# Packed attention and mixer on one core: making the last batch's packs among the first batch's products

## The chip, the cores and the metric

The kernel runs on one core of one Trainium2 chip. The metric is the device time of one execution in microseconds (us). Its engines are named as the profile names them: PE (TensorE, matmuls; PEld is its weight load), DVE (VectorE), ACT (ScalarE), POOL (GpSimd) and SP (SyncE, from whose queue all the DMAs of this kernel are issued).

## The reference

Eight batches, eight heads, 576 tokens, head dimension 64; 32 packing queries per head. Attention is done twice: the packing queries attend to keys and values and give 32 packed vectors per head, and then the real queries attend to the packed vectors. What comes out is mixed over the tokens with two thin matrices, and goes through a two-layer channel product with a relu.

```python
def _attn_ref(q, k, v, p):            # q, k, v: (8, 8, 576, 64), p: (8, 8, 32, 64)
    p_packed = sm_attn(p, k, v)       # softmax(p k^T / 8) v
    return sm_attn(q, p_packed, p_packed)

def _moe_ref(x, U, V, w_ch1, w_ch2):  # x: (8, 576, 512)
    h = x.transpose(0, 2, 1) @ U @ V  # U: (576, 32), V: (32, 576)
    u = x + h.transpose(0, 2, 1)
    ch = np.maximum(u @ w_ch1, 0.0) @ w_ch2   # (512, 2048), (2048, 512)
    return u + ch
```

U, V, w_ch1 and w_ch2 come as float64 bits; the kernel makes float32 of them on ACT and DVE.

## The kernel before, in words

**Units and packs.** The first attention is done in 16 units u = 0 to 15, two per batch, four heads each (`UN`). A unit goes through these steps, each a function: `a_load` (keys, and the packing queries with the first unit of a batch), `a_load_v` (values), `a_p` (packing queries turned, once per batch), `a_turn` (keys turned by ten PE transposes, copied out of PSUM), `a_scores` (matmuls into two banks), `a_softmax` (maximum on DVE, exponential with its sum on ACT), `a_turn_back` (five transposes of the exponentials, copied by ACT and DVE), `a_pack` (matmuls with the values; L470), `a_heads` (one transpose, and the packed vectors go to DRAM with the second unit of a batch). The loop at L505 runs these in a staggered order: in turn i it does turning back of i-1, scores of i, the turning of i+1, the pack of i-2 and the heads of i-3. Between them it converts the first weight matrix in 16 pieces and, from i = 4 on, does three steps a turn of the first batch's second attention.

**The second attention and the products.** `attention(b, res)` gives a list of 24 steps for batch b: one load of the queries, turning and scores and softmax of two halves, three steps `tokens`, `mix1` and four `mix2`. Each PE step takes one or two of two PSUM banks (pool psT, `bank()`), shared by everything. The last, `mix2`, does a matmul, an addition on DVE (L329), a copy on ACT (L330) and a subtraction on POOL (L331), and gives the pair of tiles ah and al which the products read. `fold(b, c)` multiplies a quarter of the first weight matrix by the packed vectors: eight matmuls into both banks of psT (L368), then four copies on ACT (L374) and four subtractions on DVE (L375).

The main loop (L678) runs over 8 batches and 16 rounds kt. A round is `gemm1(kt)` (12 matmuls, L86 to L88, into h_ps; relu on ACT, the low half hl on DVE at L607) and `gemm2(kt-1)` (12 matmuls into o). Products are made with three matmuls each, of high and low parts. Into a round are put: a step of the next batch's attention after `gemm1` (slot A), one after `gemm2` (slot B, where in every fourth round the fold stands instead), and in batch 0, one step between the halves of `gemm2` (slot M) for what is left of the packs. In batch 0 each round also converts one block of the second weight matrix (`load_w2`, `convert_w2`, `split_w2`): one operation on ACT, four on DVE (L78 to L81), a copy on ACT (L158) and a subtraction on POOL (L159).

**What sets the order.** Up to the line `tc.manual_schedule()` (L552) a planner orders each engine's instructions by a simulated time, so that in the first part steps may stand in another order than the code has them. Behind that line the instructions of each engine stand in the order in which the code issues them, and a slot's step waits in its engine's queue for what it needs. Tiles are in pools with a fixed count of buffers; a new tile waits until the old one of its buffer is read. The pool sA holds the keys, psA six banks of PSUM; both are closed at L548, and the products' tiles and banks take their place. sT stays open until the last `a_heads`.

Before the change all 16 units are turned, scored and exponentiated in the loop; three things are left for batch 0's slots M (`rest`, L542): the packs of units 14 and 15, the turning back of unit 15, the heads of 13, 14 and 15.

Of the kernel before, what the change touches and what calls it, by code (L numbers as in the profile page):

```python
# [8 lines left out]
F32 = mybir.dt.float32  # L9
# [10 lines left out]
def packed_attention_mixer_kernel(  # L20
# [28 lines left out]
    B, H, S, D = q.shape  # L49
# [4 lines left out]
    P = 128  # L54
    SM = 512
    NT = 9
    I = S // NT
# [98 lines left out]
    def split_w2(kt, x):  # L156
        hi, lo = w2_parts(kt)
        nc.scalar.copy(hi, x)  # L158
        nc.gpsimd.tensor_tensor(lo, x, hi.bitcast(F32), op=ALU.subtract)  # L159

    ua4 = const.tile([P, 5, 4, R], F32R, name="ua4")
    vs = const.tile([P, S], F32R, name="vs")
    nc.gpsimd.memset(ua4[I:, 4].bitcast(F32), 0.0)

    def x_tile():
        return pipe.tile([P, 5 * 2 * P], F32, name="x", tag="x", bufs=2)

    def load_uv():  # L170
        ub = x_tile()[:, :10 * R].bitcast(I32)
# [60 lines left out]
    def scores(lT, t, g, bank):  # L232

        ss = [bank() for _ in range(2)]
        for x in range(4):
            hs, h = slice(32 * x, 32 * x + 32), x ^ g
            for r in range(2):
                rs = slice(64 * r, 64 * r + 64)
                n = HALF[r].stop - HALF[r].start
                nc.tensor.matmul(ss[r][hs, :n], lhsT=lT[rs, g, hs], rhs=t[rs, h, :n], start=True, stop=True)  # L240
        return [ss[r][:, :HALF[r].stop - HALF[r].start] for r in range(2)]
# [10 lines left out]
    def attention(b, res):  # L252
# [10 lines left out]

        def turn_q(g, h):
            if h == 0:
                st["t", g] = pipe.tile([P, 4, 5 * I], F32, name="xT", bufs=1)
            turn(st["t", g], st["x", g], h, bank)

        def scores_q(g):
# [114 lines left out]
    sA = actx.enter_context(tc.tile_pool(name="sA", bufs=2, reuse_waits="tile"))  # L384
    psA = actx.enter_context(tc.tile_pool(name="psA", bufs=2, space=PSUM, reuse_waits="tile"))

    UN = [(b, g) for b in range(B) for g in range(2)]
    ua = {}
    pn, pT, pps = {}, {}, {}
# [4 lines left out]
    def a_load(u):  # L394
        b, g = UN[u]
        ua[u] = {}
        if g == 0:
            pn[b] = sA.tile([P, 2, 2, D], F32, name="pn")
            for z in range(2):
                nc.sync.dma_start(out=pn[b][:, :, z], in_=p[b].rearrange("(g h) n d -> (h n) g d", g=2))  # L400
        ua[u]["x"] = sA.tile([P, 2 * S], F32, name="kx", bufs=3)
        load_nat(ua[u]["x"], k, b, g)

    def a_load_v(u):
# [7 lines left out]

    def a_p(b):
        t_ps = bank()
        pT[b] = sA.tile([P, 2, P], F32, name="pT")
        for i in range(2):
            nc.tensor.transpose(t_ps[:, P * i:P * i + P], pn[b][:, i].rearrange("p z d -> p (z d)"), ident)
        nc.scalar.activation(pT[b][:, 0], t_ps[:, :P], AF.Copy, scale=scale)
        dst, src = (a.rearrange("p (y z n) -> p z y n", y=2, z=2) for a in (pT[b][:, 1], t_ps[:, P:2 * P]))
        for z in range(2):  # L420
            nc.scalar.activation(dst[:, z], src[:, 1 - z], AF.Copy, scale=scale)
# [6 lines left out]
        for h in range(3):  # L428
            turn(ua[u]["t"], ua[u]["x"], h, bank_a("k"))

    def a_scores(u):
        b, g = UN[u]
        ua[u]["s"] = scores(pT[b], ua[u]["t"], g, bank_a("s"))

    def a_softmax(u):
        ss = ua[u]["s"]
        mx = sA.tile([P, 3], F32, name="mx")
        sm = ua[u]["sum"] = sT.tile([P, 2], F32, name="sm", bufs=3)
        for r in range(2):
            nc.vector.tensor_reduce(mx[:, r:r + 1], ss[r], axis=AX.X, op=ALU.max, negate=True)  # L440
        nc.vector.tensor_tensor(mx[:, 2:], mx[:, :1], mx[:, 1:2], op=ALU.min)
        e1 = ua[u]["e"] = sT.tile([P, S], F32, name="e1")
        for r in range(2):
            nc.scalar.activation(e1[:, HALF[r]], ss[r], AF.Exp, bias=mx[:, 2:], accum_out=sm[:, r:r + 1])
# [57 lines left out]
            load_w1(n + 4)  # L502

    n_w1 = 0
    for i in range(NU):  # L505
        if i > 0:
            a_turn_back(i - 1, bank_a("m"))
        a_scores(i)
        if i + 1 < NU:
            a_load_v(i + 1)  # L510
            a_turn(i + 1)
        if i + 2 < NU:
            a_load(i + 2)
        a_softmax(i)
        for _ in range(2 if i in (1, 5, 9) else 1):
            if n_w1 < 16:
                some_w1(n_w1)
                n_w1 += 1
        if i > 1:
            a_pack(i - 2, bank_a("m"))  # L520
        if i > 2:
            a_heads(i - 3)
        if i >= 4:
            for _ in range(3):
                if first:
                    first.pop(0)()
        if i == 2:
            uv = load_uv()
        if i == 3:
            prepare_uv(*uv)  # L530
        if i == 12:
            load_w2(0)
            load_w2(1)
        if i == 13:
            fold(0, 0)
            steps = attention(1, res)
            steps.pop(0)()
        if i == 14:
            split_w2(*convert_w2(0))
            load_w2(2)  # L540
    assert not first
    rest = [  # L542
        lambda: (a_pack(NU - 2, bank), a_heads(NU - 3)),
        lambda: a_turn_back(NU - 1, bank),
        lambda: (a_pack(NU - 1, bank), a_heads(NU - 2)),
        lambda: (a_heads(NU - 1), tctx.close()),
    ]
    actx.close()  # L548
    split_copies = False

# [120 lines left out]
            nc.sync.dma_start(out=out[b - 1 + i].rearrange("(i c) m -> c i m", c=NT)[8], in_=os_[I * i:I * i + I])  # L671

    w2x = convert_w2(1)

    for n in (16, 15, 15, 12):
        steps.insert(n - 1, lambda: None)
    last, parts = None, []
    for b in range(B):  # L678
        cur = Batch(b)
        oj = None  # L680
        ahead = attention(b + 2, res) if b + 2 < B else []
        for kt in range(NK):
            cur.gemm1(kt)
            if oj and kt == 1:
                store_joint(b - 1, oj)
            if steps and (b == 0 or kt % 4 != 2):
                steps.pop(0)()
            if (b, kt) == (0, 5):
                w2_tiles(ctx.enter_context(tc.tile_pool(name="sC", bufs=1, side="right", reuse_waits="tile")), 2)
            if kt > 0:  # L690
                cur.gemm2(kt - 1, rest.pop(0) if rest else None)
            elif last:
                last.gemm2(NK - 1)
                last.store()
                if last.b % 2 == 1:
                    oj = joint(last.b, parts)
            if w2x:
                split_w2(*w2x)
                w2x = None
                if kt + 3 < NK:  # L700
                    load_w2(kt + 3)
                if kt + 2 < NK:
                    w2x = convert_w2(kt + 2)
            if kt % 4 == 2 and (b, kt) != (B - 1, NK - 2):
                n = b * NPC + kt // 4 + 1
                fold(n // NPC, n % NPC)
            elif steps:
                steps.pop(0)()
            if kt == 1:
                cur.blocks()  # L710
            if kt == 3:
                cur.add_u()
            if ahead and kt == 13:
                ahead.pop(0)()
            if kt == NK - 1 and b % 2 == 1:
                parts = [joint_parts(b, 0), joint_parts(b, 1)]
        assert not steps
        steps = ahead
        last = cur
# [35 lines left out]
```

## Time and profile before

| | |
|---|---|
| runs shown | 871.92, 868.63, 870.24 us; median 870.24 |
| the profiled execution | 869.67 us, of which the span of instructions is 867.1 |
| mean granted TensorE clock | 0.98 |
| DMA moved | 59.09 MB, mean 68 GB/s |
| PE / DVE / ACT / POOL busy | 829.0 / 391.6 / 330.2 / 99.3 us |

The chain of work that ended last is 82% PE, 8% DVE, 6% DMA and 2% ACT. The profile cuts the span into stretches and gives each engine's busy time in each: the first 121 us, in which packs are made and weights are converted, differ from the rest, in which the matmuls of the products follow each other. In a row of the timeline the columns are the start, the duration, the engine, the line, the operation, the tile written and the tiles read, partitions x elements, and how many; in brackets stand the idle time of the engine just before it and what ended it. A row of the waits names the waiting engine and line, what it waited for, the total, the count and the longest. A row of the chain has start, time, engine, tile and line.

### The profile page before, as it was taken

What the parts mean: (1) busy time and instruction counts of PE and PEld (TensorE: products, weight loads), DVE (VectorE), ACT (ScalarE), POOL (GpSimd) and SP (SyncE); (2) the same over time, 40 slices, a digit from 0 to 9 for tenths busy, and PEclk for the clock granted to TensorE, in tenths of its full rate; (3) what the DMA queues carried; (4) which work ended last, traced back from release to release, by engine and by line L of the source; (5) the groups of instructions that cost most, each with busy time, mean ns of one, the idle gap of its engine ahead of it and who ended that gap; (6) DMA issues with size and microseconds to landing.
All of it is one profiled execution on the core that took longest, in us unless ns stands there. A gap on an engine that the chain in (4) does not pass through costs nothing.

```text
span 867.1 us, 14707 instructions
## 1 busy us (share of the span) xinstructions
PE 829.0 (96%) x5792; PEld 659.4 (76%) x5792; DVE 391.6 (45%) x968; ACT 330.2 (38%) x1028; POOL 99.3 (11%) x128
## 2 busy tenths in 40 slices
PE   5879898989999999999999999999999999999997
PEld 2545566768888888788878878888888887888886
DVE  4689857797434423433343433434344234332221
ACT  3657664444432333234323333234323332342221
POOL 0002232333001100100010000110011001010000
PEclk8789999999999999999999999999999999999999
DMA  8999842332100110011001100011001100010001
GB/s 275 276 319 295 277 150 81 104 98 86 50 1 1 61 55 8 1 61 49 2 1 61 49 13 2 1 61 50 1 1 61 53 9 1 1 50 1 1 1 61
DMA packets 38981, 59.09 MB, mean 68 GB/s; under 512 B 11776, under 2 KB 21888, under 8 KB 38912
## 3 DMA queue, kind: packets, MB, share of 16 engines
q1 hardware_dynamic: 38912, 58.16, 21.1%
q8 instruction: 45, 0.74, 0.4%
q14 instruction: 24, 0.20, 0.1%
HBM read 47.79 MB, written 10.35 MB: 67 GB/s over the span
## 4 chain that ended last, share of the span: by engine, by line
PE 82%; DVE 8%; DMA 6%; ACT 2%; issue 1%; SPq 0%; POOL 0%; DVEq 0%; ACTq 0%
PE o L86 16%; PE o L88 16%; PE o L87 15%; PE h_ps L86 8%; PE h_ps L88 7%; PE h_ps L87 7%; PE t_ps L368 4%; DMA bits<-in_moe_w_ch_dram 2%; PE t_ps L219 2%; DVE os L80 1%; PE t_ps L240 1%; DVE os L78 1%; DMA kx<-in_k_dram 1%; PE s_ps L240 1%; PE t_ps L247 1%
## 5 line engine op out<-in xcount | busy, mean ns | idle before, releaser
L86 PE MATMUL o<-w2h,hh 128*128 128x512 f32 x512 | 206.4, 403 | 0.0
L88 PE MATMUL o<-w2h,hl 128*128 128x512 f32 x512 | 202.7, 396 | 0.0
L87 PE MATMUL o<-w2l,hh 128*128 128x512 f32 x512 | 202.3, 395 | 0.0
L607 DVE SCALAR_TENSOR_TENSOR hl<-h_ps,hh 128x256 fp32r<-128x256 f32 x256 | 104.3, 422 | 201.1 <-ACT hj L606 188.7
L604 ACT ACTIVATE hh<-h_ps 128x256 fp32r<-128x256 f32 x256 | 98.8, 388 | 181.2 <-PE h_ps L88 180.4
L86 PE MATMUL h_ps<-ah,wth 128*128 128x320 f32 (+1 forms) x512 | 158.0, 309 | 2.1 <-DVE hl L607 2.1
L87 PE MATMUL h_ps<-al,wth 128*128 128x320 f32 (+1 forms) x512 | 151.8, 296 | 0.0
L88 PE MATMUL h_ps<-ah,wtl 128*128 128x320 f32 (+1 forms) x512 | 151.6, 296 | 0.0
L86 PEld LDWEIGHTS h_ps<-ah,wth 128*128 128x128 f32 x512 | 96.9, 189 | 35.9 <-issue 27.0
L88 PEld LDWEIGHTS o<-w2h,hl 128*128 128x128 f32 x512 | 96.6, 189 | 22.8
L86 PEld LDWEIGHTS o<-w2h,hh 128*128 128x128 f32 x512 | 96.9, 189 | 20.0 <-issue 3.1
L87 PEld LDWEIGHTS o<-w2l,hh 128*128 128x128 f32 x512 | 96.9, 189 | 17.0
L87 PEld LDWEIGHTS h_ps<-al,wth 128*128 128x128 f32 x512 | 96.9, 189 | 1.7
L88 PEld LDWEIGHTS h_ps<-ah,wtl 128*128 128x128 f32 x512 | 97.1, 190 | 0.0
L375 DVE TENSOR_TENSOR wtl<-t_ps,wth 128x256 fp32r<-128x256 f32 x128 | 48.5, 420 | 92.5 <-ACT wth L374 89.1
L374 ACT CAST wth<-t_ps 128x256 fp32r<-128x256 f32 x128 | 43.5, 374 | 110.0 <-PE t_ps L368 95.7
L331 POOL TENSOR_TENSOR al<-aT,ah 128x320 fp32r<-128x320 f32 (+1 forms) x32 | 26.7, 836 | 206.5 <-ACT ah L330 206.5
L279 POOL TENSOR_TENSOR e<-e,m 128x576 f32<-128x576 f32 x16 | 19.7, 1229 | 236.6 <-DVE m L278 236.6
L368 PE MATMUL t_ps<-w1t,ppT 64*32 64x512 f32 x512 | 38.1, 601 | 0.3 <-DVE eT L455 0.2
L226 ACT COPY xT<-t_ps 128x256 f32<-128x256 f32 x60 | 20.4, 395 | 38.8 <-PE t_ps L219 38.2
L330 ACT CAST ah<-aT 128x320 fp32r<-128x320 f32 (+1 forms) x32 | 13.8, 434 | 46.5 <-DVE aT L329 46.5
L290 POOL TENSOR_TENSOR e<-e,s 128x576 f32<-128x576 f32 x16 | 18.6, 1160 | 106.2 <-DVE s L289 103.6
(130 smaller groups left out, 1009.6 us busy)
## 6 DMA issues: line engine op xcount, KB each, us to landing
bits<-in_moe_w_ch_dram SPq DMA_DIRECT2D x32, 512.0 KB, 4.8
kx<-in_k_dram SPq DMA_DIRECT2D x16, 576.0 KB, 6.5
x<-in_q_dram SPq DMA_DIRECT2D x16, 576.0 KB, 4.7
vt<-in_v_dram SPq DMA_DIRECT2D x64, 128.0 KB, 4.6
out_dram<-bits SPq DMA_DIRECT2D x32, 256.0 KB, 2.4
pn<-in_p_dram SPq DMA_DIRECT2D x16, 64.0 KB, 6.1
vt<-in_v_dram SPq DMA_DIRECT2D x16, 64.0 KB, 3.8
out_dram<-os SPq DMA_DIRECT2D x8, 128.0 KB, 2.3
```

The lines of the kernel that those rows point to most:

```text
L86: nc.tensor.matmul(ps, lhsT=lh, rhs=rh, start=start, stop=False)
L87: nc.tensor.matmul(ps, lhsT=lh, rhs=rl, start=False, stop=False)
L88: nc.tensor.matmul(ps, lhsT=ll, rhs=rh, start=False, stop=stop)
L226: nc.scalar.copy(dst, src[:, a])
L279: nc.gpsimd.tensor_tensor(e, e, m.unsqueeze(2).to_broadcast([P, S // 32, 32]), op=ALU.subtract)
L290: nc.gpsimd.tensor_tensor(e, e, s.unsqueeze(2).to_broadcast([P, S // 32, 32]), op=ALU.mult)
L331: nc.gpsimd.tensor_tensor(al[:, g, ns], aT[:, ns], ah[:, g, ns].bitcast(F32), op=ALU.subtract)
L368: nc.tensor.matmul(f_ps[g][xs], lhsT=ppT[b][zs, g, xs], rhs=w1t[h // 2][zs, QW * c:QW * c + QW], start=True, stop=True)
L374: nc.scalar.copy(hi[:, g], f_ps[g][:, cs])
L375: nc.vector.tensor_tensor(lo[:, g], f_ps[g][:, cs], hi[:, g].bitcast(F32), op=ALU.subtract)
L604: nc.scalar.activation(hh[:, ms], src, AF.Relu)
L607: nc.vector.scalar_tensor_tensor(hl[:, ms], src, 0.0, hh[:, ms].bitcast(F32), op0=ALU.max, op1=ALU.subtract)
```

## The change

The loop over units stops at 14 (`NA = NU - 2`). Units 14 and 15 (the last batch) are loaded in it, their keys into the two x tiles of the second attention, which are free once the first batch's mix is done. Their turning, scores, softmax, turning back, packs and heads become 16 steps put ahead of the second batch's attention in batch 0; the load of the second batch's queries into the same x tiles is one of them, where it stood in the loop before. Slot M is used in all of batch 0's rounds from 1 on, so that batch 0 has 43 slots for 43 steps. The first fold stands one unit earlier, the loads of the first two w2 blocks at i = 12 and 13, the conversion of the first behind the loop. In batch 1 slot A is used in every round but the first, and slot B not in the first. The load of the third batch's queries stands at the end of batch 0 in place of round 13. pT and mx move to the pool sT, whose closing comes later, so that the second half of the w2 tiles is made in round 7 in place of 5.

```diff
-        ua[u]["x"] = sA.tile([P, 2 * S], F32, name="kx", bufs=3)
+        ua[u]["x"] = sA.tile([P, 2 * S], F32, name="kx", bufs=3) if u < NA else x_tile()[:, :2 * S]
...
+    def b_turn(u, h):
+        if h == 0:
+            ua[u]["t"] = xT_tile()
+        turn(ua[u]["t"], ua[u]["x"], h, bank)
...
-    for i in range(NU):
+    for i in range(NA):
         if i > 0:
             a_turn_back(i - 1, bank_a("m"))
-        a_scores(i)
-        if i + 1 < NU:
-            a_load_v(i + 1)
+        a_scores(i, bank_a("s"))
+        if i == NA - 2:
+            load_w2(0)
+        if i == NA - 1:
+            load_w2(1)
+        a_load_v(i + 1)
+        if i + 1 < NA:
             a_turn(i + 1)
-        if i + 2 < NU:
-            a_load(i + 2)
+        a_load(i + 2)
...
         if i == 12:
-            load_w2(0)
-            load_w2(1)
-        if i == 13:
             fold(0, 0)
-            steps = attention(1, res)
-            steps.pop(0)()
-        if i == 14:
-            split_w2(*convert_w2(0))
-            load_w2(2)
     assert not first
-    rest = [
-        lambda: (a_pack(NU - 2, bank), a_heads(NU - 3)),
-        lambda: a_turn_back(NU - 1, bank),
-        lambda: (a_pack(NU - 1, bank), a_heads(NU - 2)),
-        lambda: (a_heads(NU - 1), tctx.close()),
-    ]
+    a_load_v(NU - 1)
+    a_p(UN[NA][0])
+    a_turn_back(NA - 1, bank_a("m"))
+    a_pack(NA - 2, bank_a("m"))
+    a_heads(NA - 3)
+    split_w2(*convert_w2(0))
+    load_w2(2)
+    steps = attention(1, res)
+
+    for n in (16, 15, 15, 12):
+        steps.insert(n, lambda: None)
+    u, w = NU - 2, NU - 1
+    steps = [
+        lambda: b_turn(u, 0),
+        lambda: b_turn(u, 1),
+        lambda: (a_pack(u - 1, bank), a_heads(u - 2)),
+        lambda: b_turn(u, 2),
+        lambda: (a_scores(u, bank), a_softmax(u)),
+        lambda: None,
+        lambda: (a_heads(u - 1), b_turn(w, 0)),
+        lambda: b_turn(w, 1),
+        lambda: b_turn(w, 2),
+        lambda: (a_scores(w, bank), a_softmax(w)),
+        steps.pop(0),
+        lambda: a_turn_back(u, bank),
+        lambda: a_pack(u, bank),
+        lambda: (a_turn_back(w, bank), a_heads(u)),
+        lambda: a_pack(w, bank),
+        lambda: (a_heads(w), tctx.close()),
+    ] + steps
...
-            if steps and (b == 0 or kt % 4 != 2):
+            if steps and (b < 2 or kt % 4 != 2) and (b, kt) != (1, 0):
                 steps.pop(0)()
-            if (b, kt) == (0, 5):
+            if (b, kt) == (0, 7):
                 w2_tiles(ctx.enter_context(tc.tile_pool(name="sC", bufs=1, side="right", reuse_waits="tile")), 2)
             if kt > 0:
-                cur.gemm2(kt - 1, rest.pop(0) if rest else None)
+                cur.gemm2(kt - 1, steps.pop(0) if b == 0 and steps else None)
...
-            elif steps:
+            elif steps and (b, kt) != (1, 0):
                 steps.pop(0)()
...
-            if ahead and kt == 13:
+            if ahead and kt == (13 if b else NK - 1):
                 ahead.pop(0)()
```

Not shown: `x_tile` and `xT_tile` become functions at the head, `a_scores` takes its banks as an argument, and the four empty steps (`lambda: None`) in the second batch's attention are put in here and no longer ahead of the main loop, at the same places.

More of the change, by code (lines that the diff above doesn't have):

```diff
@@ L159, in split_w2, with x_tile, xT_tile @@
         nc.gpsimd.tensor_tensor(lo, x, hi.bitcast(F32), op=ALU.subtract)
+    def x_tile():
+        return pipe.tile([P, 5 * 2 * P], F32, name="x", tag="x", bufs=2)
+    def xT_tile():
+        return pipe.tile([P, 4, 5 * I], F32, name="xT", bufs=1)
     ua4 = const.tile([P, 5, 4, R], F32R, name="ua4")
@@ L165, in packed_attention_mixer_kernel @@
     nc.gpsimd.memset(ua4[I:, 4].bitcast(F32), 0.0)
-    def x_tile():
-        return pipe.tile([P, 5 * 2 * P], F32, name="x", tag="x", bufs=2)
     def load_uv():
@@ L265, in turn_q @@
             if h == 0:
-                st["t", g] = pipe.tile([P, 4, 5 * I], F32, name="xT", bufs=1)
+                st["t", g] = xT_tile()
             turn(st["t", g], st["x", g], h, bank)
@@ L385, in packed_attention_mixer_kernel @@
     psA = actx.enter_context(tc.tile_pool(name="psA", bufs=2, space=PSUM, reuse_waits="tile"))
+    NA = NU - 2
     UN = [(b, g) for b in range(B) for g in range(2)]
@@ L414, in a_p @@
         t_ps = bank()
-        pT[b] = sA.tile([P, 2, P], F32, name="pT")
+        pT[b] = sT.tile([P, 2, P], F32, name="pT")
         for i in range(2):
@@ L429, in a_turn, with a_scores @@
             turn(ua[u]["t"], ua[u]["x"], h, bank_a("k"))
-    def a_scores(u):
+    def b_turn(u, h):
+        if h == 0:
+            ua[u]["t"] = xT_tile()
+        turn(ua[u]["t"], ua[u]["x"], h, bank)
+    def a_scores(u, bank):
         b, g = UN[u]
-        ua[u]["s"] = scores(pT[b], ua[u]["t"], g, bank_a("s"))
+        ua[u]["s"] = scores(pT[b], ua[u]["t"], g, bank)
     def a_softmax(u):
         ss = ua[u]["s"]
-        mx = sA.tile([P, 3], F32, name="mx")
+        mx = sT.tile([P, 3], F32, name="mx")
         sm = ua[u]["sum"] = sT.tile([P, 2], F32, name="sm", bufs=3)
@@ L673, in packed_attention_mixer_kernel @@
     w2x = convert_w2(1)
-    for n in (16, 15, 15, 12):
-        steps.insert(n - 1, lambda: None)
     last, parts = None, []
```

## The prediction

> **What bounds the kernel now.** I read the stretches of the span (columns: length, busy time of PE, PEld, DVE, ACT and POOL with instruction counts, PEclk, DMA share, GB/s), then PE's waits inside the first batch.
>
> ```profile
> 10.00:95.00 85.00, 68.30 (x800) 42.09 (x794) 70.21 (x203) 50.03 (x150) 9.39 (x15) 0.82 0.96 298
> 95.00:121.10 26.10, 23.84 (x359) 13.39 (x357) 16.83 (x51) 17.97 (x59) 8.71 (x16) 0.93 0.82 251
> 121.10:217.10 96.00, 88.65 (x633) 69.97 (x626) 71.84 (x138) 46.89 (x134) 29.66 (x30) 1.00 0.28 87
> 217.10:303.00 85.90, 85.62 (x550) 70.36 (x549) 33.74 (x83) 30.91 (x99) 8.43 (x10) 1.00 0.08 28
> ...
> PE t_ps L219 <- DVE wtl L375: 2.7, 1, 2.7
> PE h_ps L86 <- DVE hl L607: 2.1, 3, 1.2
> PE t_ps L247 <- DVE wtl L375: 2.0, 1, 2.0
> ```
>
> There are three regimes. Until 95 us the DMA engines are 0.96 busy, and the change touches nothing there. From 95 to 121 us the last packs are made; no engine is full, and it is a chain of small steps on four engines. From 121.1 us the products run: batch 1 takes 85.9 us with PE busy throughout, batch 0 takes 96.0 us. Batch 0 carries two packs, one turning back and three heads more than batch 1 (3.2 us by the rows below); the other 6.9 us are waits, and the three named ones make 6.8. The time of the kernel is therefore the start of the first product plus the length of batch 0 plus a tail (batches 1 to 7) that the change leaves alone: batch 1 has 26 slots for its 23 steps (24 before), and the load of the third batch's queries still waits for the same mix, which ends before it. So the forecast is a difference of two numbers.
>
> **The start of the first product.**
>
> ```profile
> 107.17 0.74 PE L240 MATMUL s_ps<-kT,pT 64*32 64x320 f32 x8
> 107.84 0.95 PE L219 MATMUL k_ps<-ident,kx 128*128 128x128 f32 x4
> 109.36 1.08 PE L240 MATMUL s_ps<-kT,pT 64*32 64x256 f32 x8
> 110.64 1.01 PE L219 MATMUL k_ps<-ident,kx 128*128 128x128 f32 x4
> 116.18 0.84 PE L470 MATMUL m_ps<-vt,eT 128*32 128x64 f32 x36
> 120.30 0.90 PE L470 MATMUL m_ps<-vt,eT 128*32 128x64 f32 x40
> 121.13 0.42 PE L86 MATMUL h_ps<-ah,wth 128*128 128x320 f32 x1
> ...
> 107.83 2.12 POOL L331 TENSOR_TENSOR al<-aT,ah 128x256 fp32r<-128x256 f32 x2 [0.41 <-ACT ah L330]
> ...
> 112.47 0.15 DVE L441 TENSOR_TENSOR mx<-mx 128x1 f32<-128x1 f32 x1
> ...
> 113.09 0.52 ACT L444 ACTIVATE e<-s_ps,mx 128x320 f32<-128x320 f32 x1
> 113.59 0.47 ACT L444 ACTIVATE e<-s_ps,mx 128x256 f32<-128x256 f32 x1
> ```
>
> The scores at 107.17 and 109.36 are unit 13's, the last that stays ahead of the products. Today the pack of unit 13 (120.30) ends the stage; after the change the last pack there is that of unit 12 (116.18 today, done at 117.0). If nothing else moved, the product would start at 117.0, 4.1 us earlier: the late bound. But unit 13's scores are cut in two by the transposes of unit 15's keys (107.84), and its maximum (112.47) and exponentials (113.09) come after more of them (110.64) and their copies. Without these 0.95 + 1.01 us of PE and the copies I put the second half of the scores near 108.4, the maximum at 110, the exponentials (113.09 to 114.1 today, 1.0 us) at 110 to 111, the turning back and pack 12 (0.7 + 0.84) behind: a start at 112.0, **9.1 us earlier**. The early bound is the first batch's own attention: its last al ends at 107.83 + 2.12 = 109.95 and the first product reads it in its second half, so with handoffs about 110.4, 10.7 us earlier. My value lies nearer the early bound because the unit behind which the steps queued is gone. The first fold, moved ahead by one unit, is then off this chain.
>
> Loads: keys 14 and 15 now wait for the attention tiles, which the mix frees near 99 us; their first use is a step behind the first product, after 112, and a load takes 6.5 us:
>
> ```profile
> kx<-in_k_dram SPq DMA_DIRECT2D x16, 576.0 KB, 6.5
> ```
>
> Queued behind them on SP stand values and the second w2 block, which the products need only in batch 0's third round. The second batch's queries are issued at the eleventh step (round 4) and used at the seventeenth (round 6), two rounds of 85.9/16 = 5.4 us at least, against 6.5 for a load of the same size. These edits I cost at nothing; with the cover gone, a late w2 block holds ScalarE, whose order is fixed, for up to 3 us (in the range, not in the sum).
>
> **The work that moves into batch 0.**
>
> ```profile
> 122.99 0.45 PE t_ps L219 x4
> 126.32 0.22 PE t_ps L229 x2
> 127.93 0.87 PE t_ps L470 x40
> 145.89 0.26 PE t_ps L480
> ...
> 130.35 0.76 PE L240 MATMUL t_ps<-xT,ppT 64*32 64x320 f32 x16
> 134.14 0.60 PE L247 MATMUL t_ps<-ident,e 128*128 128x128 f32 x4
> 134.58 0.27 PE L249 MATMUL t_ps<-ident,e 128*64 128x128 f32 x1
> ```
>
> These are the same operations at batch 0's clock. Two units are turned (each 2 x 0.45 + 0.22 = 1.12) and scored (0.76): 3.76 us. Turning back unit 14 costs 0.44 + 0.27 = 0.71, the pack of unit 13 0.87, one more head 0.26. Sum **5.6 us**, all on PE, which is the bound there: nothing hides it. DVE gains two maxima and a turning back, about 2.5 us on its 71.84; ACT about 7 us on its 46.89: neither becomes full on average.
>
> **The waits in batch 0.** The two t_ps banks serve every step, and the fold takes both until its last wtl. Behind that, PE's next step waits:
>
> ```profile
> 143.04 0.63 PE L219 MATMUL t_ps<-ident,x 128*128 128x128 f32 x4 [2.72 <-DVE wtl L375]
> ...
> 103.69 0.82 DVE L440 TENSOR_REDUCE mx<-s_ps 128x1 f32<-128x320 f32 x2 [0.95 <-PE s_ps L240]
> 123.28 0.27 ACT L481 COPY ppTa<-t_ps 128x128 f32<-128x128 f32 x1 [1.07 <-DMA ppTd<-ppTa]
> 123.44 0.39 ACT L604 ACTIVATE hh<-h_ps 128x256 fp32r<-128x256 f32 x1
> 124.08 0.70 ACT L226 COPY xT<-t_ps 128x256 f32<-128x256 f32 x2
> 130.39 1.61 ACT L585 CAST rdh<-ppall 32x64 fp32r<-32x64 f32 x8
> 132.03 0.30 ACT L588 CAST ajh<-ah 128x128 fp32r<-128x128 f32 x1
> 133.57 0.43 DVE e L272
> 134.00 0.33 DVE e L273
> 137.46 1.06 PE L368 MATMUL t_ps<-w1t,ppT 64*32 64x512 f32 x8 [0.22 <-DVE eT L455]
> ```
>
> Counting slots (43 steps on 43 slots): after the fold of round 2 comes a turn of unit 15 in place of a turn of the queries, so the 2.7 stays. After round 6's fold came a step without a bank, now comes a turn; after round 10's came tokens (the 2.0), now comes a step without a bank. So the 2.0 moves and the sum of both stays. New is round 2: the banks of the first deferred scores are freed by an exponential that waits for the maximum, which DVE takes up where it takes the e transposes today, at 133.57, behind a w2 conversion. Maximum (0.82 + 0.15) and exponentials (1.0) put ACT at 135.5, where the banks come free at 134.3 today; with handoffs 135.7. ACT then still has the block copies (1.61 + 0.3), the next two hh (0.8) and the copies of the waiting head and turn (0.27 + 0.7): 139.4 instead of the 137.46 at which the fold's second half began: **+2.0**. New too is the end: the last mix step now stands directly ahead of batch 1's first product.
>
> ```profile
> 106.61 0.75 DVE L329 TENSOR_TENSOR aT<-t_ps,aT 128x256 f32<-128x256 f32 x2
> 107.33 0.73 ACT L330 CAST ah<-aT 128x256 fp32r<-128x256 f32 x2
> ```
>
> Its chain is add 0.38, copy 0.37, al 1.06 (halves of 0.75, 0.73 and 2.12) and PE's own 0.3 to 0.4, about 2.2 us; a product's twelve matmuls take 122.99 - 121.13 = 1.86 us, and the eleventh reads that al, 1.5 us in: **+0.7**. The waits on hl (2.1) come where DVE is back to back; PE now has 3 us more of its own work in those rounds, so I take half away: **-1.0**. Bounds for the three together: -4.1 (both the 2.0 and the 2.1 vanish) to +7.8 (three more waits of this kind, as in the bank rival below, and the end).
>
> **Sum.** -9.1 + 5.6 + 2.0 + 0.7 - 1.0 = -1.8 us. The profiled execution took 869.67 us (span 867.1); the median of the runs shown is 870.24, 0.6 above it and inside their spread. Forecast: 869.67 - 1.8 = **867.9 us**, which no measurement of this kernel would tell from no change: it can tell about 0.5%, 4.35 us, that is below 865.9 or above 874.6.
>
> **The clock as a rule would have it.**
>
> ```profile
> 90.00:100.00 10.00, 9.42 (x119) 7.16 (x123) 7.35 (x21) 6.71 (x21) 0.24 (x1) 0.83 0.81 261
> 140.00:150.00 10.00, 7.28 (x83) 6.07 (x82) 6.03 (x13) 4.89 (x14) 1.53 (x2) 1.00 0.16 57
> ```
>
> The stretch with the 2.72 us wait kept a granted clock of 1.00; before the products it fell to 0.83. If a longer wait let it fall so in batch 0, ten us of products would cost 10 x (1/0.83 - 1) = 2.0 us more. The Trainium skill, "TensorE: Matmul & The Clock Gate", section "Why this matters for your kernels", speaks against the change here: it warns of gaps of over about 3 us between bursts of matmuls, after which the clock falls back to half. The 2.72 us gap agrees with it, and the trace of before shows no longer one among the products. By that page's window of about 3.4 us at half rate, an estimate, one longer gap would cost 1.7 us, and the sum would be -0.1.
>
> **The rivals.**
> Faster, 861.2: the start reaches its early bound (-10.7) and the added PE work covers DVE's backlog, so that the waits of 2.0 and 2.1 go: -10.7 + 5.6 - 4.1 + 0.7 = -8.5. For it: DVE is only 75% busy in batch 0 and the rounds get longer. Against: the waits follow from the order in the queues, not from load. Chance 0.28.
> Slower, 873.9: the banks. With three steps a round, five places (rounds 2, 3, 7, 9, 13) instead of two wait for a bank that DVE frees behind a w2 conversion, at 2.35 us each (mean of 2.7 and 2.0): 11.75 instead of 4.7, so -9.1 + 5.6 + 7.05 + 0.7 = +4.2. It decides from the second added wait on (-2.8 + 4.7 is above zero). For it: the two rows; against: only folds and scores take both banks. Chance 0.17.
> The change doesn't do what it says: the planner of the first part puts the same steps ahead of the product, and it starts at 117.0 only: -4.1 + 7.3 = +3.2, 872.9. Chance 0.12.
> The clock falls in batch 0: -1.8 + 2.0, 869.9. Chance 0.04.
> The forecast: 0.39, its own range 865 to 872.
>
> **How the numbers follow.** Below 865.9 lie nearly all of the faster rival (0.27) and a tenth of the forecast (0.04): 0.31. Above 874.6 lie half of the bank rival (0.09), the late start with any further wait (0.06) and a late w2 block (0.05): 0.20. The rest, 0.49, is the same. The range from 860.5 to 876 takes in the early bound with the covered waits and the bank rival with a start two us later; both mishaps together (878) are left out.
>
> **What would show it.** Right: first product at 110 to 115 us; batch 0 at 101 to 106 us between its first product and batch 1's; a wait of 2 to 3 us on wtl in rounds 3 and 7 and none in round 11; a wait on the first fold's banks in round 2; under 1.5 us at batch 1's first product; batches 1 to 7 unchanged within 0.5 us. Wrong: a start after 117, a batch 0 above 108 or below 99, or a clock under 1.00 in it.

## The result and the profile after

The changed kernel takes 876.13 us (median of 6 runs, 874.36 to 878.37), the kernel before 871.75 (6 runs, 868.63 to 873.88): a ratio of **1.0054** with a 95% interval of 1.0028 to 1.0079. It is slower by half a per cent, 8.2 us above the forecast of 867.9 and just over the upper end of the range. The profiled execution took 874.36 us with a span of 872.6, against 869.67 and 867.1: 5.5 us longer in span.

The windows of the changed kernel (same columns as in the prediction). The first product now starts at 114.64, and batch 1 at 221.91:

```profile
10.00:95.00 85.00, 66.91 (x864) 41.26 (x863) 72.28 (x210) 52.76 (x160) 9.94 (x16) 0.94 0.96 303
95.00:102.00 7.00, 4.73 (x69) 2.29 (x68) 6.80 (x14) 4.03 (x15) 2.92 (x3) 1.00 0.89 286
102.00:110.00 8.00, 7.15 (x39) 2.11 (x39) 3.53 (x11) 3.53 (x11) 2.27 (x3) 0.57 0.64 226
...
114.64:221.91 107.27, 95.18 (x730) 74.46 (x723) 72.39 (x146) 52.03 (x149) 30.29 (x34) 0.98 0.29 96
221.91:308.47 86.56, 85.94 (x550) 70.72 (x549) 34.47 (x86) 30.76 (x100) 9.51 (x12) 1.00 0.08 28
```

Until 95 us the DMA engines are 0.96 busy as before, and PE 66.91 us (68.30). Between 95 and 102 us PE has little to do (4.73 of 7.00) at a clock of still 1.00; behind that the clock falls. Four numbers hold the whole difference; the tail behind batch 1 is the rest of the span:

| | before | after | difference | forecast |
|---|---|---|---|---|
| start of the first product | 121.13 | 114.64 | -6.5 | -9.1 |
| batch 0 | 95.96 | 107.27 | +11.3 | +6.6 |
| batch 1 | 85.90 | 86.56 | +0.7 | +0.7 |
| tail | 564.11 | 564.13 | 0.0 | 0 |

So two terms failed, by 2.6 and by 4.7 us, both in the same direction. In batch 0 PE's busy time grew by 6.5 us (88.65 to 95.18) and its idle time by 4.7 (7.35 to 12.09). The waits of PE, batch 0 first and then batch 1 (waiting line, what it waited for, total, count, longest):

```profile
PE h_ps L86 <- DVE hl L636: 3.0, 2, 1.6
PE t_ps L222 <- DVE wtl L378: 2.6, 1, 2.6
PE t_ps L232 <- DVE wtl L378: 2.0, 1, 2.0
PE t_ps L371 <- DVE e L275: 1.1, 1, 1.1
PE t_ps L319 <- DVE x L312: 1.0, 1, 1.0
PE t_ps L490 <- ACT e L454: 1.0, 1, 1.0
PE t_ps L371 <- ACT ppTa L491: 0.6, 1, 0.6
PE t_ps L490 <- ACT eT L462: 0.6, 1, 0.6
...
PE h_ps L87 <- POOL al L334: 0.4, 1, 0.4
```

The two waits on wtl stand where the prediction put them, in rounds 3 and 7, and none is left in round 11. But six waits of batch 0 are new or larger. The second surprise is the granted clock, 0.57 between 102 and 110 us, where the packs are ending. There a gap of 2.46 us on PE stands ahead of matmuls that then take nearly twice their time. PE, DVE and POOL in that place:

```profile
93.52 1.22 PE L319 MATMUL t_ps<-x,ua 128*128 128x256 f32 x8 [0.25 <-ACT ppTa L491]
...
98.01 1.27 POOL L159 TENSOR_TENSOR w2l<-os,w2h 128x512 fp32r<-128x512 f32 x1 [3.63 <-ACT w2h L158]
98.05 1.51 DVE L79 TENSOR_SCALAR os<-os 128x512 int32<-128x512 int32 x1
...
99.23 1.05 POOL L334 TENSOR_TENSOR al<-aT,ah 128x320 fp32r<-128x320 f32 x1
99.59 1.24 DVE L80 SCALAR_TENSOR_TENSOR os<-bits,os 128x512 int32<-128x512 int32 x1
100.86 0.69 DVE L81 SCALAR_TENSOR_TENSOR os<-bits,os 128x512 int32<-128x512 int32 x1
101.47 0.82 DVE L450 TENSOR_REDUCE mx<-s_ps 128x1 f32<-128x320 f32 x2
102.20 0.81 DVE L332 TENSOR_TENSOR aT<-t_ps,aT 128x320 f32<-128x320 f32 x2
102.74 0.40 PE L331 MATMUL t_ps<-vs,ms 128*128 128x256 f32 x1 [2.46 <-DVE aT L332]
...
103.66 1.93 PE L371 MATMUL t_ps<-w1t,ppT 64*32 64x512 f32 x8
...
106.13 1.29 PE L243 MATMUL s_ps<-kT,pT 64*32 64x320 f32 x8
...
114.64 0.41 PE L86 MATMUL h_ps<-ah,wth 128*128 128x320 f32 x1
```

The addition at L332, for which PE waits, stands in DVE's queue behind the conversion of a w2 block (L79 to L81) and a maximum. The eight matmuls of the fold (103.66) take 1.93 us; in the kernel before this form took 1.06. The matmul with ua at 93.52 (`mix1` of the first batch) serves as a mark below; the kernel before has it at 97.02.

### The profile page after: what moved, and what is told of

Read it like the earlier page. It is cut to its first block, busy times and chain, and to the rows that moved or that the text cites. A ratio compares the mean times of both kernels' runs of the same rounds, so it can differ in the third digit from the quotient of the medians.

```text
span 872.6 us, 14714 instructions
## 1 busy us (share of the span) xinstructions
PE 825.9 (95%) x5792; PEld 656.4 (75%) x5792; DVE 389.2 (45%) x964; ACT 330.6 (38%) x1032; POOL 99.6 (11%) x128
## 4 chain that ended last, share of the span: by engine, by line
PE 84%; DVE 7%; DMA 3%; ACT 2%; issue 1%; SPq 1%; POOL 0%; DVEq 0%; ACTq 0%
PE o L86 16%; PE o L88 16%; PE o L87 16%; PE h_ps L86 8%; PE h_ps L87 7%; PE h_ps L88 7%; PE t_ps L371 4%; PE t_ps L222 2%; DMA bits<-in_moe_w_ch_dram 1%; PE t_ps L243 1%; DVE os L80 1%; DVE os L78 1%; PE s_ps L243 1%; PE t_ps L250 1%; DVE os L79 1%
## 5 line engine op out<-in xcount | busy, mean ns | idle before, releaser
L334 POOL TENSOR_TENSOR al<-aT,ah 128x320 fp32r<-128x320 f32 (+1 forms) x32 | 25.9, 812 | 192.4 <-ACT ah L333 170.6
L229 ACT COPY xT<-t_ps 128x256 f32<-128x256 f32 x68 | 23.1, 394 | 42.8 <-PE t_ps L222 41.9
L78 DVE TENSOR_SCALAR os<-os 128x512 f32<-128x512 f32 (+2 forms) x35 | 20.7, 593 | 23.5 <-ACT os L77 20.2
```

What stands on the lines that cost most here:

```text
L78: nc.vector.tensor_single_scalar(t, t, LEAST, op=ALU.max)
L229: nc.scalar.copy(dst, src[:, a])
L334: nc.gpsimd.tensor_tensor(al[:, g, ns], aT[:, ns], ah[:, g, ns].bitcast(F32), op=ALU.subtract)
```

## The experiments

The theories, with the letters that the expectations use where they use any. For batch 0: the main theory is DVE's order. In a round the conversion of a w2 block (four operations, some 3 us) is issued ahead of slot B and the fold, so that wtl, the maxima and the copies that free PSUM banks queue behind it. The rivals: the waits are DVE's load and only move (L), or the moved PE work itself costs more than 5.6 us. For the start: the first fold, one unit earlier, stands ahead of unit 13's scores (F); the conversion of a w2 block, on DVE ahead of the additions that PE waits for, holds the stage (V); PE has too little to do at the end of the pack stage and its clock falls (C).

**Batch 0: the order of DVE's queue, and no conversion at all.** `after_conv_last` and `before_conv_last` issue the conversion behind slot B or the fold, in the kernel after and in the kernel before:

```diff
-            if w2x:
+            more = w2x is not None
+            if more:
                 split_w2(*w2x)
                 w2x = None
                 if kt + 3 < NK:
                     load_w2(kt + 3)
-                if kt + 2 < NK:
-                    w2x = convert_w2(kt + 2)
...
+            if more and kt + 2 < NK:
+                w2x = convert_w2(kt + 2)
             if kt == 1:
                 cur.blocks()
```

> The changed kernel with one edit: in each round of batch 0 the conversion of the next w2 block (ACT L77, DVE L78 to L81) is issued behind slot B or the fold instead of ahead of it; nothing is left out. Theory Q (order in the queue): what frees the two t_ps banks (wtl, the e transposes, the maxima) stands behind a conversion of some 3 us on DVE, so PE's waits on wtl (2.6 + 2.0), e (1.1), the exponential (1.0) and tl (1.0) shrink from 7.7 us to under 2, batch 0 goes from 107.3 to about 101 us, and the time falls by about 6 us. Rival L (load): DVE is simply behind in batch 0, the waits move to hl (3.0 now, then 8 or more), and batch 0 stays at 106 to 108 us.

> The kernel before with the same edit as after_conv_last; nothing is left out. Theory Q: its waits on wtl (2.7 + 2.0) go, batch 0 falls from 96.0 to about 91.5 us, the time by 4 to 5 us; since the changed kernel had more such waits, the two kernels with the edit differ by some 2 us less than the 4.4 us of the two without it. Rival L: batch 0 stays at 95 to 97 us.

`after_nodve` and `before_nodve` leave DVE's four operations of the conversion out in batch 0 (one operation of ACT per block stays, and the products are of other numbers), so that the difference of the two batches 0 is the moved work without these waits:

```diff
     def convert_w2(kt):
+        if kt >= 2:
+            x = conv_tile(F32)
+            nc.scalar.activation(x, bits.pop(("w2", kt))[:, :, 1].bitcast(F32), AF.Abs)
+            return kt, x
```

> The changed kernel without DVE's four operations for each of the w2 blocks 2 to 15 (the block is then the absolute value of the high words, so the products are of other numbers); ACT's, POOL's and PE's work stays. Some 40 us of DVE work leave batch 0. If the conversions cause the added waits (Q and L both), PE's waits in batch 0 fall under 2 us and batch 0 is its PE work, 85.9 + 3.2 + 5.6, that is 94.7 to 96.5 us. Rival D (density): three steps a round on two banks wait for each other whatever DVE does; then waits of 4 us or more stay and batch 0 is above 99 us.

> The kernel before without DVE's four operations for the w2 blocks 2 to 15 (the same part left out as in after_nodve). Batch 0 falls from 96.0 to its PE work, 85.9 + 3.2, that is 89 to 91 us. The difference of after_nodve's batch 0 to this one prices the moved PE work by itself: 5.6 us as I worked it out; 8 or more would say that the moved steps cost more on PE than their matmuls.

Measured, all beside the same runs of the kernel before (872.48): after_conv_last 870.21 us, ratio 0.9971 [0.9953, 0.9990]; before_conv_last 867.52, 0.9930 [0.9904, 0.9957]; the nodve kernels 862.67 and 861.59 (one run each). Batch 0 and PE's largest waits in it, in after_conv_last (98.78 us):

```profile
120.71:219.49 98.78, 92.76 (x730) 73.04 (x724) 67.57 (x146) 52.51 (x149) 30.06 (x34) 1.00 0.33 105
...
PE h_ps L86 <- DVE hl L636: 4.4, 4, 1.5
PE t_ps L490 <- ACT eT L462: 0.6, 1, 0.6
```

and in before_conv_last (93.25):

```profile
122.58:215.83 93.25, 88.48 (x631) 69.87 (x626) 65.14 (x138) 46.63 (x134) 29.09 (x30) 1.00 0.28 89
...
PE h_ps L86 <- DVE hl L607: 3.5, 4, 1.7
PE t_ps L368 <- DVE aT L329: 0.9, 1, 0.9
```

One edit takes 8.5 us out of the changed kernel's batch 0 (107.27 to 98.78) and 2.7 out of the other's. The waits on wtl, e and x are gone. L is right in one part: those on hl rise, from 3.0 to 4.4 and from 2.1 to 3.5. How the order makes the largest wait is seen in round 3, POOL, DVE and PE of the changed kernel:

```profile
132.12 1.29 POOL L159 TENSOR_TENSOR w2l<-os,w2h 128x512 fp32r<-128x512 f32 x1 [8.17 <-ACT w2h L158]
132.65 1.05 DVE L78 TENSOR_SCALAR os<-os 128x512 f32<-128x512 f32 x1 [1.31 <-ACT os L77]
133.80 0.43 DVE L79 TENSOR_SCALAR os<-os 128x512 int32<-128x512 int32 x1
134.26 0.69 DVE L80 SCALAR_TENSOR_TENSOR os<-bits,os 128x512 int32<-128x512 int32 x1
134.99 0.69 DVE L81 SCALAR_TENSOR_TENSOR os<-bits,os 128x512 int32<-128x512 int32 x1
135.60 1.61 DVE L378 TENSOR_TENSOR wtl<-t_ps,wth 128x256 fp32r<-128x256 f32 x4
...
137.02 1.02 PE L222 MATMUL t_ps<-ident,x 128*128 128x128 f32 x4 [2.56 <-DVE wtl L378]
```

The four wtl start only when the conversion, 3 us long, is done. In after_conv_last they go first:

```profile
138.41 1.60 DVE L378 TENSOR_TENSOR wtl<-t_ps,wth 128x256 fp32r<-128x256 f32 x4
140.16 0.43 DVE L78 TENSOR_SCALAR os<-os 128x512 f32<-128x512 f32 x1
```

The edit does one thing more than change the order. L78 takes 1.05 us in the first of these views, where it meets POOL's L159 (the subtraction of the block before), begun ahead of it, and 0.43 in the second. So it is in most rounds (columns behind the count: shortest, median and longest in ns; first the kernel after, then after_conv_last):

```profile
L78 DVE TENSOR_SCALAR os<-os x14: 364/1036/1117, 118.8 to 208.8; 128x512 f32<-128x512 f32 x14
L78 DVE TENSOR_SCALAR os<-os x14: 365/428/1171, 125.4 to 207.9; 128x512 f32<-128x512 f32 x14
```

The four operations of the 14 conversions together take 41.4 us of DVE in the changed kernel's batch 0 and 35.6 in after_conv_last, 43.1 in the kernel before and 36.1 in before_conv_last. Order and shorter conversions were not tried apart. In round 3 the order must be the larger part, since a conversion shorter by 0.62 us would have left most of the 2.56. And 1.6 of the 8.5 us are the clock of round 3, taken up below: in an execution without that fall the changed kernel's batch 0 took 105.70 us, and the edit is worth 6.9 against it.

The moved work is priced twice: without DVE's operations batch 0 takes 92.52 us after and 87.03 before, 5.5 more; with the conversion last 98.78 and 93.25, again 5.5. That speaks against the rival that it costs more than the forecast's 5.6.

**The start: three theories.** `after_warm` adds 64 transposes of the identity that nobody reads, 32 in each of the last two turns of the loop over units; `after_fold_late` puts the first fold back; `after_w2_late` loads the first two w2 blocks a unit later still; `after_all` has these two and the conversion last.

```diff
+        if i >= NA - 2:                                     # after_warm
+            for _ in range(8):
+                idle = bank_a("k")()
+                for j in range(4):
+                    nc.tensor.transpose(idle[:, P * j:P * j + P], ident, ident)
...
-        if i == 12:                                         # after_fold_late
+        if i == 13:
             fold(0, 0)
...
-        if i == NA - 2:                                     # after_w2_late
+        if i == NA - 1:
             load_w2(0)
-        if i == NA - 1:
-            load_w2(1)
...
+    load_w2(1)
     a_load_v(NU - 1)
```

> The changed kernel with idle PE work at the end of the pack stage: 64 transposes of the identity into k_ps banks that nobody reads, given to the planner in units 12 and 13 (about 7 us of PE at full clock). Theory C (clock): in the changed kernel the stage's end has too little PE work, PE's granted clock falls to 0.5 to 0.7 between 100 and 110 us, and that is why the first product starts at 114.6 and not at 112; then with the idle transposes the clock stays above 0.9 from 95 us to the first product, and it starts no later, at 110 to 114, although PE does more. Rival W (work and waits): the start is set by the chain through DVE and ACT or by PE's work; then it is the same or later by what the transposes take, 115 to 121, whatever the clock.

> The changed kernel with the first fold given to the planner at i = 13 in place of 12; nothing is left out. In the profile of the changed kernel the fold's eight matmuls stand ahead of unit 13's scores and take 1.9 us, and four more in the midst of them. Theory F: this puts the fold on the chain to the first product, which starts 1.5 to 2.5 us earlier without it (112 to 113), batch 0 unchanged within 0.5 us. Rival: the chain is the maximum and exponential of unit 13 and the clock, and the start moves by less than 1 us.

> The changed kernel with the first two w2 blocks loaded a unit later each (i = 13 and behind the loop); nothing is left out. In the changed kernel DVE converts the first block from 98 to 101.5 us while the first mix's additions wait behind it and PE waits 2.5 us for them. Theory V: without it the additions come 2 to 3 us earlier, PE has no such gap, the clock stays higher, and the first product starts 1.5 to 3 us earlier than 114.6; the conversions then fall into batch 0's first rounds, which get up to 2 us longer. Rival: the start stays at 114 to 116 and batch 0 grows by the late conversions.

> The changed kernel with three edits together: conversions behind slot B in batch 0, the first fold at i = 13, the first two w2 blocks loaded a unit later; nothing is left out. If Q, F and V hold together: first product at 111 to 113, batch 0 at 98.8 to 100 us, time 864 to 866 us, below the kernel before with its conversions moved (867.5). If only Q holds: start at 114 to 120, time 867 to 871.

Measured, beside 871.12 us: after_warm 874.78, 1.0044 [1.0019, 1.0069]; after_fold_late 878.50, 1.0085 [1.0054, 1.0116]; after_w2_late 876.04, 1.0067 [1.0043, 1.0092]; after_all 870.08, 0.9993 [0.9970, 1.0015]. The first product started at 115.23, 117.34, 117.63 and 115.73 us. F falls: with the fold behind unit 13's scores the start was no earlier, nor, counted from the mark (96.10), the way shorter (21.2 us against 21.1). V isn't decided: the way was 20.7 us (mark at 96.96), but a conversion, in both traces that of the second w2 block, still stood on DVE ahead of the addition, and PE's gap stayed:

```profile
105.91 0.39 PE L331 MATMUL t_ps<-vs,ms 128*128 128x256 f32 x1 [2.19 <-DVE aT L332]
```

after_all, with both, needed 21.25 us from its mark, and its batch 0 took 98.78, as in after_conv_last. With 64 transposes the clock was 1.00 and the way from the mark 18.0 us, but the mark came at 97.22 in this execution.

**Fewer idle transposes.** `after_warm_half` has 24 of them (`range(3)`), `conv_warm_half` the same with the conversion last. `before_conv_warm` is before_conv_last with 48 (`range(3)` from i = 12 on), to see whether the clock held the kernel before as well. `one_conv_last` moves only the last unit (`NA = NU - 1`, 13 leading steps), with the conversion last.

> The changed kernel with 24 idle transposes at the end of the pack stage in place of 64 (2.6 us of PE at full clock in place of 7). With 64 the clock was 1.00 and the chain to the first product was PE alone, a third of it the idle transposes. Theory C (clock): with fewer the clock still stays above 0.8 from 100 us on, and the first product starts at 111 to 113; the time falls by 2 to 4 us against the changed kernel. Rival W: the idle work was covered and the start is set by DVE and ACT; then it is 114 to 117 whatever the clock.

> The changed kernel with the conversions behind slot B in batch 0 and the same 24 idle transposes. If C and Q add up: start at 111 to 113, batch 0 at 98.8, time 863 to 866 us. If the clock falls all the same: start 115 to 121, time 868 to 872.

> The kernel before with the conversions behind slot B and 48 idle transposes (12 in each of units 12 to 15; 5.3 us of PE at full clock). Control for the clock: the stage's end of the kernel before has the transposes of two more units in its gaps. If its clock still costs it time, the first product starts at 119 to 121.5 (122.6 without); if PE's work and not its clock sets the start there, it comes 1 to 5 us later, at 123.5 to 127, and the time rises from 867.5 by as much.

> Half the change: only unit 15 is made among the products (unit 14 stays ahead of them), with the conversions behind slot B in batch 0. Its moved PE work is one turn and one scoring, 1.9 us, where two units moved 5.5 us. Theory T (trade): the products pay the moved PE work in full, so batch 0 is 93.25 + 1.9 = 95 to 96 us, and the start gains by about half of what two units gave (some 4.7 us between the two kinds of kernels so far): 119 to 120.5; time 866 to 869, no different from the kernel before with the same edit (867.5). Rival: the last unit alone holds the start, which then comes at 116 to 118, and the time is 863 to 866.

Measured, beside 869.71 us: 873.95, 1.0053 [1.0031, 1.0075]; 868.13, 0.9973 [0.9949, 0.9998]; 867.94, 0.9979 [0.9961, 0.9998]; 873.33, 1.0029 [0.9999, 1.0060]. The first two are the cleanest look at the clock, since they do the same up to the first product. Their windows from the mark to that product, first after_warm_half:

```profile
94.81:112.55 17.74, 15.56 (x231) 10.01 (x231) 13.05 (x36) 11.96 (x41) 7.01 (x12) 1.00 0.74 250
```

and conv_warm_half:

```profile
96.64:116.69 20.05, 18.62 (x232) 10.51 (x232) 13.14 (x36) 12.06 (x41) 7.02 (x12) 0.83 0.62 205
```

The same work (231 and 232 recorded matmuls) took 2.3 us longer at a clock of 0.83 than at 1.00. So 24 transposes do not always keep the clock. Whether the clock holds the kernel before as well stays open. With 48 transposes its clock was 1.00 and the stretch 25.48 us, but PE was busy for 24.22 of these, the transposes among them; without them it had 0.93 in two executions (24.11 and 23.35 us) and 0.86 to 0.87 in three (24.43 to 25.30). Its total time gained nothing (867.94 against 867.52 for before_conv_last). one_conv_last was expected at 866 to 869 and missed; it settles nothing: the first product came at 121.02, its batch 0 took 100.01 us, and its own layout of slots made new waits (7.1 us on hl).

**More of them, and the two kernels again.** `conv_warm_mid` has 40 transposes (`range(5)`) and the conversion last, `conv_warm_full` 64. `after_again` and `before_again` are the two kernels unchanged, one run each, to see how the start scatters.

> The changed kernel with the conversions behind slot B in batch 0 and 40 idle transposes in the pack stage (24 left the clock at 0.64 from 105 to 114.5 us). Theory C: the clock stays above 0.9, the first product starts at 112 to 114.5, batch 0 takes 98.8, time 863 to 866 us, below the kernel before with the same conversion edit (867.5). Rival W: the start is 115 to 118 and the time 867 to 870 whatever the clock.

> The same with 64 idle transposes, with which the clock was 1.00 in after_warm and the first product came at 115.2, PE alone being the chain. Theory C: clock 1.00, start 114 to 116, time 865 to 867.5.

> The changed kernel once more, as it is: how far the start of its first product scatters between executions (114.6 in its first profile, at a clock of 0.52 from 105 to 110 us). Its median time is 1.8 us above that profile's, so I expect 115 to 118; batch 0 within 0.3 us of 107.3. Were the scatter of batch 0 as large as that of the start, the terms could not be told apart by single profiles.

> The kernel before once more, as it is: first product at 120.5 to 123.5 (121.1 in its first profile), batch 0 within 0.3 us of 96.0.

Measured, beside 870.17 us: conv_warm_mid 865.55, 0.9938 [0.9914, 0.9962]; conv_warm_full 865.48, 0.9943 [0.9919, 0.9966]; after_again 874.56, before_again 871.46. Batch 0 took 96.36 us in before_again, near the first profile (95.96), but 105.70 in after_again, 1.6 less than in the first profile and outside the expectation. With the runs so far the start comes apart into two pieces, the time of the mark and the stretch behind it (all from the timelines; the clock is the granted one of that stretch):

| | mark | first product | stretch | clock |
|---|---|---|---|---|
| before | 97.02 | 121.13 | 24.11 | 0.93 |
| before_again | 99.89 | 123.24 | 23.35 | 0.93 |
| after | 93.52 | 114.64 | 21.12 | 0.84 |
| after_again | 95.89 | 116.42 | 20.53 | 0.83 |
| after_w2_late | 96.96 | 117.63 | 20.67 | 0.83 |
| after_conv_last | 97.80 | 120.71 | 22.91 | 0.70 |
| after_nodve | 94.61 | 117.56 | 22.95 | 0.70 |
| after_warm | 97.22 | 115.23 | 18.01 | 1.00 |
| conv_warm_mid | 96.82 | 114.31 | 17.49 | 1.00 |

In the kernels with the change the stretch follows the clock: 17.5 to 18.0 us at 1.00, 20.5 to 21.1 at 0.83 to 0.84, 22.9 at 0.70. The runs left out fit in: 21.24 at 0.84 (after_fold_late), 21.25 at 0.76 (after_all), 17.74, 18.01 and 17.49 at 1.00 (after_warm_half, conv_warm_full, conv_warm_mid_5). This supports C, with one reserve: all those at 1.00 have idle transposes, which also put some DVE operations in another order, so only the pair above prices the clock alone. The mark scatters by four microseconds among executions of the same instructions (93.52 in after, 97.80 in after_conv_last); where that comes from, in the 0.96 busy DMA engines or elsewhere, wasn't tried.

**The last pair, on one chip.** Best version of the changed kernel against the best of the kernel before, five rounds:

> conv_warm_mid (the changed kernel, conversions behind slot B, 40 idle transposes) against the kernel before with the conversion edit alone, on one chip. From the terms: start 114.3 against 122.6, batch 0 98.8 against 93.3, batch 1 86.6 against 85.9, so 2.1 us less, 0.25%: with five rounds the two intervals should just about touch. If the moved packs are worth nothing even so, the two medians agree within 1 us.

> The kernel before with the conversions behind slot B, again, for the comparison with conv_warm_mid_5: 867 to 868 us, a ratio to the kernel before of 0.993 to 0.996; batch 0 at 93.3 us.

Measured, beside 870.59 us: conv_warm_mid again 866.68, 0.9948 [0.9930, 0.9966]; before_conv_last again 866.64, 0.9948 [0.9925, 0.9970]. Equal, where 2.1 us less were expected of the first. In it the products start 5.4 us earlier (116.66 against 122.03; stretch again 17.49), its batch 0 is 5.6 longer (98.74 against 93.16), its batch 1 0.7 (86.59 against 85.90). Both beat both kernels by about half a per cent or more; before_conv_last does so with one edit and without the moved packs.

## Why the prediction was wrong, step by step

**The start** was put at 112.0 and came at 114.64: the step "a start at 112.0, 9.1 us earlier" was mis-sized. It took the mark where the kernel before has it (97.02) and left 15.0 us behind it. Measured were 21.1. Of the 6.1 too many, 2.3 are the clock (priced by the pair above), 1.1 are the rest of the way from 20.05 to 21.1, where after has the 2.46 us wait behind DVE's conversion and conv_warm_half waits of 0.21 and 0.60, and 2.7 remain at a clock of 1.00 (17.7 against 15.0). This split is an estimate: the 17.7 holds 24 idle transposes, and no run had the clock at 1.00 without any. So how much of the 2.7 is the chain of unit 13's softmax, turning back and pack 12, taken too short, stays open. More than half of the error was hidden by luck, since the mark came 3.5 us earlier in this execution. The sentence "The first fold, moved ahead by one unit, is then off this chain" isn't what the timeline shows, where the fold stands on PE ahead of unit 13's scores, but it has no price: moving it back gained nothing.

**The clock** was a rival at a chance of 0.04, and placed in batch 0 only. It fell at both places, and a clock under 1.00 in batch 0 (0.98) was one of the prediction's own signs of being wrong. At the end of the packs, 24.11 us with 21.85 busy at a clock of 0.93 became 21.12 with 16.94 at 0.84, the slowed matmuls included. The change takes PE work out of this stage: without idle transposes seven executions of the changed kernel and its variants had a clock of 0.70 to 0.84 there, five of the kernel before and its variants 0.86 to 0.93. The idle transposes, which put some work back, raised it again. In batch 0, the 2.56 us wait of round 3 was followed by this (the window behind it, changed kernel):

```profile
137.00:140.40 3.40, 3.38 (x10) 2.67 (x11) 0.94 (x3) 1.10 (x5) 0.00 (x0) 0.52 0.92 324
```

and in after_again, the same kernel, the same wait, by this:

```profile
138.80:142.20 3.40, 3.38 (x18) 2.70 (x18) 0.94 (x3) 2.21 (x8) 0.14 (x1) 1.00 0.97 318
...
138.82 0.63 PE L222 MATMUL t_ps<-ident,x 128*128 128x128 f32 x4 [2.58 <-DVE wtl L378]
```

Ten matmuls against eighteen in 3.4 us; round 3 took 13.24 us against 11.67, 1.6 more. The four other runs that leave batch 0 as it is bear this out: after_fold_late, after_warm and after_warm_half had a clock of 0.50 to 0.56 behind this wait and a batch 0 of 107.14 to 107.19, after_w2_late 1.00 and 105.64. The prediction let the 2.72 us gap of the kernel before, at a clock of 1.00, stand for the safety of gaps of that length. The Trainium skill, "TensorE: Matmul & The Clock Gate", section "Why this matters for your kernels", warns of gaps over about 3 us. Here the clock fell behind gaps of 2.46 and 2.56, and not behind 2.58 and 2.72; a wait of 2.57 was followed by 0.51 in after_warm_half and by 1.00 in after_w2_late, and in conv_warm_half the clock fell at the end of the packs with no wait over 0.60. The same page of the Trainium skill, in its Part 1, says that the window by which the gate judges runs freely, so that a kernel differs from execution to execution by its phase; after and after_again agree with that.

**The moved work**, 5.6 us: right, 5.5 measured twice.

**The waits in batch 0.** Right: wtl in rounds 3 and 7 (2.6 and 2.0 against 2.7 and 2.0). Round 2: a wait on the exponential as described, but smaller (1.0 and then 0.6 on ppTa; the round is 1.5 longer, against +2.0). Wrong: "I take half away" of the waits on hl. They grew from 2.1 to 3.0. The two of the changed kernel, at the starts of rounds 12 and 13, come behind a conversion on DVE whose L79 and L80 take about 1.2 and 1.7 us, beside operations of POOL; so did the two larger ones of the kernel before, at the starts of rounds 9 and 10. New is that the fold's four wtl (1.61 us) also stand ahead of the first of them. Missed: the fold of round 10 waits for e behind a conversion (1.1), `mix1` in round 14 for x (1.0), a head for eT (0.6). The step that failed is therefore the counting of slots: it followed only the two waits that the trace of before shows, and not each new step that needs DVE in a round where a conversion is issued ahead of it. The bank rival (873.9) had this mechanism with too high a price: 2.35 us at each of five places, where the new ones (rounds 2, 5, 10 and 14) cost 0.6 to 1.6.

**The account of batch 0.** Beyond the forecast are 1.9 for hl (3.0 in place of 1.1), 1.1, 1.0, 0.6 and, for the clock, 1.6; 0.4 less came in round 2 and 0.1 in the moved work, and 0.4 of small waits of the kernel before are gone. That is 5.3 for the 4.7 us by which batch 0 overran. The 0.6 between lie in PE's busy time (5.5 and 1.6 make 7.1, and it grew by 6.5); where they went stays open.

**The end**: right. 0.4 us of wait at batch 1's first product, and batch 1 0.66 longer.

**The planner** rival fell (a start of 114.64, not 117.0), and the late w2 blocks cost nothing that a run showed. The faster rival fell too: PE's waits in batch 0 didn't go, they rose from 7.2 to 11.9 us.

## What to carry to other kernels

Before work is moved from a sparse stage into a dense one, look at what it leaves behind: the moved work costs its full time in the dense stage (5.5 us here), while the sparse stage can give back less than the chain promises; one reason here was that the engine that got idler there lost its clock (2.3 us between the pair above). Before steps are added to a round, see which job of the shared engine is issued ahead of the copies that free the banks; putting a 3 us job that nobody waits for behind them gained 2.7 us in the kernel before and 6.9 to 8.5 in the changed one. And a forecast that is the difference of two large terms should carry the errors of both: here 2.6 and 4.7 us around a forecast of -1.8.

## What was not expected of the hardware

Work that nobody needs can keep the clock up: with 24 to 64 transposes of an identity it was 1.00 behind the mark in six of seven profiled executions (24 failed once, in conv_warm_half), and without them in none of thirteen (0.70 to 0.93). A gap alone doesn't decide it, and one execution doesn't tell what the next will do.

DVE was slowed beside POOL in the stretch quoted first. L79 takes 0.43 us at 133.80, but 1.51 at 98.05, when POOL's L159 had begun 0.04 us earlier: POOL ended at 99.28, and 0.43 behind that is 99.71, against a measured end of 99.56. The Trainium skill, "SBUF — State Buffer", section "SBUF: two separate sides", says that GpSimd shares a pair of ports with DVE operations in a two-port mode or with two inputs in SBUF, that whichever starts first holds it for its whole instruction, and that the other blocks; the row agrees to within 0.15 us. L80 fits in the same way with POOL's L334, the subtraction of the mix: it ended at 100.28, 0.69 behind that is 100.97, and L80 ended at 100.83. So two operations of POOL added some 1.6 us (1.08 at L79, 0.55 at L80) to the very DVE queue that PE was waiting for.
